# An attention-plus-FFN kernel whose engine orders are written out by a list scheduler in the kernel, with fp32 loads cast on Pool, batch 0 taken pair by pair, and four shared PSUM buffers

## The chip, the cores and the metric

One core of one Trainium2 chip. The metric is the device time of one execution in microseconds (us). Every execution has a state: "slow" when it is over 1.5% above the fastest of the same kernel, otherwise "fast". Engine names are those of the profile: PE (TensorE matmul), PEld (its weight load), DVE (VectorE), ACT (ScalarE), POOL (GpSimd), SP (SyncE, which here only issues DMAs; SPq is its queue).

## The reference

Block-sparse attention over 4 batches, 8 heads, 768 positions and 64 values a head, followed by a feed-forward network (FFN) on the 3072 x 512 result.

```python
scores = scale * q @ k.T                      # per batch and head
mask   = neighbours | first/last block | sampled_blocks   # blocks of 32
attn   = softmax(where(mask, scores, -1e9)); x = attn @ v
h = x @ w_in                                  # 3072 x 1024
e = exp(h - max); solu = h * e / sum(e)
ln = (solu - mean) / sqrt(var + 1e-6) * g_ln
out = ln @ w_out                              # fp32, 3072 x 512
```

Both kernels work in bf16. The mask is added by the score matmul itself: 24 extra rows of the transposed k hold a block selector ("selp" rows) and 24 extra rows of the transposed q hold the block mask ("mskp" rows). So no score can be computed before a short chain of small operations has built the mask from `sampled_blocks`. The layer norm's mean is folded into w_out once, at the start ("w_out preparation": scale by g, column sums on PE, scale and subtract).

The work comes in units of (batch, tile of 256 queries, pair of heads). A unit has 3 score tiles, 3 exps of 128x1024 and one P·V accumulation with a normalisation (`r`, `x`). Four units of one (batch, tile) give the x of one FFN block. There are 48 units, 144 exps and 12 FFN blocks.

## The kernel before

Tile buffers and their waits are handled by the framework; the order of instructions on each engine is the order of the program text.

```python
def load_pair(b, pr):                 # q, k, v of two heads: cast by the Pool's DMA
    for src, nm in ((k, "kc"), (q, "qc")):
        t = ld.tile([P, NCH, 2, D], BF16, tag=nm, name=nm)
        for hh in range(2):
            nc.gpsimd.dma_start(out=t[:, :, hh, :],
                in_=src[b, 2 * pr + hh, :, :].rearrange("(p c) d -> p c d", p=P))
    ...                               # v likewise
# ... mask chain: affine_selects on Pool, then on DVE samp_lo, eq, anyeq, maskT,
#     mskb, and the two permuted copies selp and mskp
def transpose_pair(b, pr):            # 6 PE transposes each of k and q, copied out by DVE
    ...
def prep_w1():                        # DVE: w_out_g[c] = w_out_f[c] * g[c], 8 times
def prep_w2():                        # PE column sums, then DVE, 8 times:
    nc.vector.scalar_tensor_tensor(out=w_out_sb[:, c, :], in0=w_out_f[:, c, :],
        scalar=g_sb[:, c:c+1], in1=wbar, op0=ALU.mult, op1=ALU.subtract)
# ... PSUM: 2 score tiles, 2 tiles "h", 2 tiles "m" for all else
units = [(b, t, pr) for b in range(B) for t in range(NT) for pr in range(NPR)]
for u, (b, t, pr) in enumerate(units):
    ...                               # loads and transposes of the next batch
    for n in range(3):
        scores(b, t, pr, n, exs)      # 4 matmuls, 1 exp
        if n == 0 and prev is not None:
            pv(*prev)
            # a finished (b, t) appends its FFN pieces to bg
        if bg: bg.popleft()()         # one FFN piece between score tiles
```

The softmax here doesn't subtract the row's maximum and nothing guards it: scores larger than these inputs give would overflow.

## Time and profile before

| | kernel before |
|---|---|
| time, median of 4 runs | 282.58 us (281.29 to 283.04) |
| profiled span | 281.1 us, clock 0.997 |
| first score matmul | 24.96 us |
| first FFN block's input copied (xT) | 50.94 us |
| PE busy | 85% |

The page of the kernel before. In the rows of 40 digits one digit is a fortieth of the span (7.0 us) and gives the busy share in tenths; the queue line gives packets, MB and the share of the 16 DMA engines' time; the last line is the chain of work that ended last, by engine.

```profile
span 281.1 us, 7445 instructions
PE 238.8 (85%) x3163; PEld 183.2 (65%) x3177; DVE 157.9 (56%) x365; ACT 174.4 (62%) x206; POOL 82.8 (29%) x142
...
PE   0116686999999999999999999999999999899783
...
ACT  1002468548858859667677688588488595785630
...
DMA  5999999409759810049279020090100200200202
...
q0 software_dynamic: 55056, 10.49, 45.8%
...
PE 62%; DMA 11%; ACT 10%; DVE 9%; issue 3%; POOL 3%; ACTq 0%; POOLq 0%
```

Seven slices of start, 27 in which PE is busy 90% or more, and a short end. The timeline of the same kernel (start, duration, engine, line, operation; "x8" is eight in a row; in brackets how long the engine was idle and what ended it):

```profile
2.21 0.12 DVE L110 CAST samp_lo<-samp_i 1x72 bf16<-1x72 int32 x1
...
13.11 0.80 PE L161 MATMUL tp<-ident,kc 128*128 128x128 bf16 x6 [10.51 <-DMA kc<-in_k_dram]
...
18.65 0.65 DVE L138 COPY selp<-sel 24x768 bf16<-24x768 bf16 x1
...
22.99 0.65 DVE L138 COPY mskp<-mskb 24x768 bf16<-24x768 bf16 x1
...
24.96 1.91 PE L215 MATMUL s<-qT_87,kT_85 88*128 88x256 bf16 x8
...
34.14 3.80 DVE L192 TENSOR_SCALAR w_out_g<-w_out_f,g_sb 128x512 bf16<-128x512 f32 x8
...
42.93 5.37 DVE L203 SCALAR_TENSOR_TENSOR w_out_sb<-w_out_f,g_sb,wbar 128x512 bf16<-128x512 f32 x8
```

The first k load releases PE at 13.11 us, the mask chain ends at 23.6 us, the first score follows at 24.96 us. Four durations here matter later: the undisturbed samp_lo takes 0.12 us, selp and mskp take 0.65 us each, and the two halves of the w_out preparation 3.80 and 5.37 us.

**How full is PE?** Busy PE is not full PE, so I count work. From gap-free pieces of this trace: 8 score matmuls take 0.89 us, 24 P·V matmuls 0.75, 8 h matmuls 0.875, 8 output matmuls 1.74, 8 statistics matmuls 0.20. The Trainium skill, "TensorE: Matmul & The Clock Gate" (section "Wait — 56ns, not 53.3ns?") gives N / 2.4 GHz plus about 2.5 ns from one warm matmul to the next, from which I estimate 109.2 ns for 256 columns; the trace agrees with 0.875 / 8 = 109.4 ns. A transpose of 128 columns is taken as 0.056 us by the same formula (an estimate). Work in a stretch is the number of weight loads of each kind in it times these paces, 216 us for the whole program; "lost" is the length of the stretch minus its work. These are estimates, good to about a microsecond.

| kernel before | length | work | lost |
|---|---|---|---|
| 0 to 66 us | 66 | 29.2 | 36.8 |
| 66 to 238 us | 172 | 155.6 | 16.4 |
| 238 to 281.1 us | 43.1 | 31.5 | 11.6 |

### The profile page before, as it was taken

To read this page: it belongs to the slowest core of one execution; us is meant where nothing else is said; L and a number is where in the kernel's file an instruction comes from. 1 tells how busy PE (TensorE), PEld (TensorE's weight loads), DVE (VectorE), ACT (ScalarE), POOL (GpSimd) and SP (SyncE) were. 2 spreads that over 40 slices of the span, in tenths; PEclk is the share of its full clock that TensorE was granted. 3 is DMA by queue.
4 is the path that set the end of the run, shared out by engine and by line. 5 is a ranking of instruction groups with operands and counts; after the bars stand their busy time and mean duration, and the time that the engine had idled before them with its cause. 6 is when DMAs were issued, how large, how long until landed. Compare 5 with 4: busy or idle time off the path is not lost.

```text
span 281.1 us, 7445 instructions
## 1 busy us (share of the span) xinstructions
PE 238.8 (85%) x3163; PEld 183.2 (65%) x3177; DVE 157.9 (56%) x365; ACT 174.4 (62%) x206; POOL 82.8 (29%) x142
## 2 busy tenths in 40 slices
PE   0116686999999999999999999999999999899783
PEld 0004564867867867867767768678678577686561
DVE  3079789648639622756666616386376236155261
ACT  1002468548858859667677688588488595785630
POOL 8695861218139110045253100140100101001001
PEclk9999999999999999999999999999999999999998
DMA  5999999409759810049279020090100200200202
GB/s 117 264 191 188 185 180 118 58 4 140 48 93 128 85 54 23 2 90 100 30 109 79 3 77 2 37 96 2 47 31 2 77 2 2 76 2 3 76 0 77
DMA packets 61636, 20.40 MB, mean 73 GB/s; under 512 B 52225, under 2 KB 56994, under 8 KB 61602
## 3 DMA queue, kind: packets, MB, share of 16 engines
q0 software_dynamic: 55056, 10.49, 45.8%
q1 hardware_dynamic: 6546, 9.43, 9.8%
q8 instruction: 25, 0.41, 0.6%
q14 instruction: 9, 0.07, 0.1%
HBM read 23.07 MB, written 6.29 MB: 104 GB/s over the span
## 4 chain that ended last, share of the span: by engine, by line
PE 62%; DMA 11%; ACT 10%; DVE 9%; issue 3%; POOL 3%; ACTq 0%; POOLq 0%
PE s L215 15%; PE h L268 15%; PE ops L304 14%; PE op L231 10%; ACT ex L220 8%; DMA kc<-in_k_dram 7%; PE s3p L283 6%; DMA vc<-in_v_dram 4%; DVE w_out_sb L203 2%; ACT ot L312 2%; PE tp L161 2%; POOL qc L73 1%; DVE xT L258 1%; PE tps L256 1%; DVE x L240 1%
## 5 line engine op out<-in xcount | busy, mean ns | idle before, releaser
L220 ACT ACTIVATE ex<-s 128x1024 bf16<-128x1024 f32 x144 | 141.1, 1024 | 68.9 <-PE s L215 67.8
L215 PE MATMUL s<-qT_87,kT_85 88*128 88x256 bf16 (+1 forms) x288 | 49.5, 284 | 5.8 <-ACT ex L220 3.1
L231 PEld LDWEIGHTS <-ex 128*128 128x128 bf16 x1152 | 45.7, 98 | 11.1 <-ACT ex L220 4.6
L268 PE MATMUL h<-xT,w_in_sb 128*128 128x256 bf16 x384 | 47.8, 272 | 1.3 <-DVE xT L258 0.6
L215 PE MATMUL s<-qT_88,kT_86 88*128 88x256 bf16 (+1 forms) x288 | 46.2, 272 | 2.0 <-ACT ex L220 1.2
L273 DVE TENSOR_TENSOR solu<-h,e 128x512 bf16<-128x512 f32 x48 | 33.0, 687 | 26.3 <-ACT e L272 26.2
L304 PE MATMUL ops<-w_out_sb,solu 128*128 128x512 bf16 x179 | 44.6, 378 | 0.9 <-DVE s_4734 L290 0.3
L268 PEld LDWEIGHTS <-w_in_sb 128*128 128x128 bf16 x384 | 37.0, 97 | 6.3 <-issue 1.6
L272 ACT ACTIVATE e<-h 128x512 bf16<-128x512 f32 x48 | 28.7, 598 | 18.1 <-PE h L268 16.9
L215 PEld LDWEIGHTS <-kT_85 88*128 88x128 bf16 (+1 forms) x288 | 27.3, 101 | 13.5 <-issue 6.0
L73 POOL DMA_DIRECT2D kc<-in_k_dram x32 | 26.8, 841 | 18.6 <-PE tp L161 17.7
L215 PEld LDWEIGHTS <-kT_86 88*128 88x128 bf16 (+1 forms) x288 | 26.0, 97 | 9.3 <-issue 4.0
L304 PEld LDWEIGHTS <-solu 128*128 128x128 bf16 x192 | 18.4, 97 | 18.1 <-issue 0.3
L73 POOL DMA_DIRECT2D qc<-in_q_dram x32 | 26.2, 822 | 8.0 <-DMA w_in_sb<-in_moe_w_in_dram 3.7
L231 PE MATMUL op<-va_92,ex 128*128 128x65 bf16 x576 | 26.2, 193 | 2.7 <-ACT ex L220 2.2
L231 PE MATMUL op<-va_91,ex 128*128 128x65 bf16 x576 | 25.2, 196 | 1.9 <-DVE x L240 1.0
L239 DVE RECIPROCAL r<-op 128x4 f32<-128x4 f32 x48 | 8.5, 180 | 30.8 <-PE op L231 29.3
L274 DVE TENSOR_TENSOR sq<-solu 128x512 bf16<-128x512 bf16 x48 | 20.4, 425 | 1.3
L240 DVE TENSOR_TENSOR x<-op,r 128x256 bf16<-128x256 f32 x48 | 20.1, 420 | 1.0
L161 PE MATMUL tp<-ident,kc 128*128 128x128 bf16 x96 | 9.2, 240 | 12.2 <-DMA kc<-in_k_dram 10.5
L309 DVE TENSOR_SCALAR ot<-ops,rs 128x512 f32<-128x512 f32 x12 | 9.0, 751 | 16.7 <-PE ops L304 12.7
L312 ACT ACTIVATE ot<-ops,rs 128x512 f32<-128x512 f32 x12 | 8.2, 687 | 14.3 <-PE ops L304 14.3
(127 smaller groups left out, 201.7 us busy)
## 6 DMA issues: line engine op xcount, KB each, us to landing
out_dram<-ot SPq DMA_DIRECT2D x24, 256.0 KB
kc<-in_k_dram POOLq DMA_DIRECT2D x32, 96.0 KB, 5.1
qc<-in_q_dram POOLq DMA_DIRECT2D x32, 96.0 KB, 4.4
vc<-in_v_dram POOLq DMA_DIRECT2D x16, 192.0 KB, 5.0
w_out_f<-in_moe_w_out_dram SPq DMA_DIRECT2D x1, 2048.0 KB
w_in_sb<-in_moe_w_in_dram POOLq DMA_DIRECT2D x1, 1024.0 KB, 9.5
kT_86<-selp SPq DMA_DIRECT2D x8, 36.0 KB
qT_88<-mskp SPq DMA_DIRECT2D x8, 36.0 KB
```

The lines of the kernel that those rows point to most:

```text
L73: nc.gpsimd.dma_start(out=t[:, :, hh, :], in_=src[b, 2 * pr + hh, :, :].rearrange("(p c) d -> p c d", p=P))
L161: nc.tensor.matmul(tp[:, c * P : (c + 1) * P], src[:, c, :, :], ident, is_transpose=True, start=(c == 0), stop=(c == NCH - 1))
L215: nc.tensor.matmul(s[:, m, :], kT[i][rows[hh], hh, pr, jc * P : (jc + 1) * P], qT[i][rows[hh], hh, pr, t * TW : (t + 1) * TW], start=(m % ...
L220: nc.scalar.activation(out=e, in_=s, func=ACT.Exp, scale=scale)
L231: nc.tensor.matmul(op[:, qt, hh, :], exs[n][:, m, qt * P : (qt + 1) * P], va[i][:, 2 * pr + hh, jc, :], start=first, stop=(n == 2 and m == ...
L240: nc.vector.tensor_tensor(out=x[:, :, 2 * pr * D : (2 * pr + 2) * D].rearrange("p a (h d) -> p a h d", h=2), in0=op[:, :, :, 0:D], in1=r.b ...
L268: nc.tensor.matmul(h[:, ff, :], w_in_sb[:, c, f * P : (f + 1) * P], st["xT"][:, c, :], start=(ff == 0 and c == 0), stop=(ff == 1 and c == ...
L272: nc.scalar.activation(out=st["e"][:, sl, :], in_=h, func=ACT.Exp)
L273: nc.vector.tensor_mul(out=st["solu"][:, sl, :], in0=h, in1=st["e"][:, sl, :])
L274: nc.vector.tensor_mul(out=st["sq"][:, sl, :], in0=st["solu"][:, sl, :], in1=st["solu"][:, sl, :])
L283: nc.tensor.matmul(s3p[:, qt, g : g + 1], st[nm][:, f, qt * P : (qt + 1) * P], onesf[:, 0:1], start=first, stop=(qt == 1 and g == 2 and f ...
L304: nc.tensor.matmul(ops, st["solu"][:, f, qt * P : (qt + 1) * P], w_out_sb[:, f, :], start=(f == 0), stop=(f == KF - 1))
```

## The change

Intent: start earlier, and leave PE no bubbles. Every instruction becomes an `op` with an estimated duration, dependencies and a due date (in units of exps). A greedy list scheduler gives each engine its order, and the kernel emits that order. Loads are plain fp32 DMAs with 1536-byte rows issued by SP, cast afterwards on Pool. (The Trainium skill, "DMA: Bandwidth & Descriptors", section "SWDGE vs HWDGE vs iDMA", says that only a DMA issued from Pool can cast on the way.) In batch 0 a pair of heads is used for all three tiles before the next pair is needed. The four PSUM buffers that are not for scores are shared by everything.

```diff
+class Plan:
+    def run(self):                       # greedy: the engine that can start first goes on
+        ...
+                for o in ops:
+                    t, slot = self.place(o)
+                    if t == INF: continue
+                    key = (max(t, now), o.due) if t > now + 0.02 else (now, o.due)
+                    if pick is None or key < pick[0]: pick = (key, o, slot, max(t, now))
-    ps_h = ctx.enter_context(tc.tile_pool(name="ps_h", bufs=2, space=PSUM))
-    ps_m = ctx.enter_context(tc.tile_pool(name="ps_m", bufs=2, space=PSUM))
+    mbank = [psum.tile([P, 2, TW], FP32, name=f"mbank{i}") for i in range(4)]
-            nc.gpsimd.dma_start(out=t[:, :, hh, :], in_=src[b, 2 * pr + hh, :, :]...)
+        stage[(which, b, pr)] = op("SP", 0.08, lambda o: nc.sync.dma_start(
+            out=dst[o.slot].rearrange("p h c d -> p h (c d)"),
+            in_=src[b, 2 * pr : 2 * pr + 2]...), due=-50 + len(loads), ...)
+            ca = op("POOL", pool_us(S), cast, [ld], due=due, ...)     # pool_us(768) = 0.89
+    zeros[(nm, i)] = op("POOL", ..., memset of kT/qT of the other pairs, due=-30 + 40 * i)
+    mask_rows[0].append(op("DVE", ..., rows of pairs 1 to 3 copied, due=-30))
+    w_out_f = (eso ... .bitcast(FP32))   # the fp32 w_out lies where e and solu come later
+    wg = [op("DVE", dve_us(d_model, 2), ..., due=20) for c in range(KF)]
+    wo = [op("DVE", dve_us(d_model), ..., [wb], due=28) for c in range(KF)]
-units = [(b, t, pr) for b in range(B) for t in range(NT) for pr in range(NPR)]
+units = [(0, t, pr) for pr in range(NPR) for t in range(NT)]
+units += [(b, t, pr) for b in range(1, B) for t in range(NT) for pr in range(NPR)]
+            feed(b, t, lambda f, j=j: 37 + 9.8 * (j + f))   # due dates of the FFN pieces
+    order = plan.run()
+    with tc.manual_schedule():
+        for o in order: o.emit(o)
```

## The prediction

> **What bounds it now.** The profile page has PE busy 85% of 281.1 us, ACT 62%, DVE 56%, POOL 29%; the chain of waits is 62% PE, 11% DMA. Two stages differ.
>
> Start (0 to 50 us): by the windows only 221 of 3163 matmuls have begun by 50 us. In the timeline the first scores start at 24.9 us: the first k load, cast by a Pool DMA in 256-byte pieces (q0: 55056 packets, 45.8% of the DMA engines' time), releases PE at 13.1 us, and the mask chain waits behind other DVE work until 18.6 us. Scores then stutter (16 of 144 exps by 50 us) on loads, mask-row DMAs, DVE copies and a 5.3 us w_out block on DVE.
>
> After 50 us PE is 94 to 98% busy in the windows, but busy PE is not full PE: one (batch, tile) block repeats every 19.1 to 19.9 us in the chain. Gap-free pieces in the timeline: 8 score matmuls 0.89 us, 24 PV 0.75, 8 h 0.875, 8 output 1.74, 8 stats 0.20. My estimate of all PE work from these: 144x0.445 + 48x0.75 + 48x0.875 + 24x1.74 + 72x0.20 + transposes about 16 + 2 = 216 us. So some 65 us are lost: 35 to 40 at the start, about 20 in bubbles (19.2 against about 17.5 per block), about 7 at the end.
>
> **What the change does.** (1) Loads become hardware-queue DMAs with 1536-byte rows; 80 Pool DMA issues of 0.72 to 0.84 us (64 us of Pool) go, 46 Pool casts of 768 columns come. The Pool select of 768 columns took 1.01 us, so about 48 us: off the path. The Trainium skill, "SBUF — State Buffer" (who interferes with whom) says a Pool op and a two-port DVE op exclude each other; no line of this trace shows it, but I expect some DVE ops (squares, casts) to lengthen. DVE has 40% idle. (2) The mask chain comes first, memsets move to Pool: first scores at about 9 us (estimate: load landed about 4, cast, transposes, about 8 us of DVE work). (3) Batch 0 pair by pair: each pair gives 9 exps. Back-to-back exps run at 0.92 us (5 in 4.69), so the 30 exps before the first FFN block end at about 9+28 = 37 us, ACT-bound, PE having done about 25 us of its work. (4) The order spreads FFN pieces between scores evenly, and four shared PSUM buffers replace 2+2: bubbles shrink.
>
> **Sum.** 37 + (216-25) + 6 for the last block's latency and output DMA + 5 of remaining bubbles = 239 us. ACT after 37 us needs only 114x0.92 + 48x0.5 + 12x0.6 = 136 us, so PE bounds the rest. Of the 43 us gained, about 25 come from the start, 15 from bubbles, the rest from the tail.
>
> Predicted 239 us; 230 to 251 holds it 8 times in 10. Faster by over 2%: 0.96; within 2%: 0.03; slower: 0.01.
>
> **What would show each step.** First score at 8 to 11 us. ACT nearly gapless to about 37 us, with PE about half used, then PE over 95% in every slice. Block repeat 16.5 to 17.8 us. Chain: PE 75 to 80%, DMA under 5%, ACT 10% or more at the start. Pool casts 0.9 to 1.2 us. Under-512-byte packets fall from 52225 to a few thousand. Matmul and exp durations unchanged, clock about 1.0.
>
> **What would make it wrong.** Pool casts much slower than 1 us (staging buffers and SP's in-order queue stall loads, and outputs behind them); DVE blocked by Pool, delaying solu and so PSUM release; the fixed order built on durations that differ from the chip's, so that an in-order engine waits where another order would not (blocks stay at 19 us: about 255); a first score later than 9 us.

## The result

| | before | changed |
|---|---|---|
| time, median of 4 runs | 282.58 us | 257.42 us (256.93 to 259.12) |
| profiled span, clock | 281.1 us, 0.997 | 255.2 us, 0.99 |
| first score matmul | 24.96 us | 16.95 us |
| first xT copy | 50.94 us | 65.92 us |
| PE busy | 85% | 88% |

The ratio is 0.9128 (0.9085 to 0.917). A ratio is the mean time of one kernel's fast runs over that of the other's of the same rounds, so it is not quite the ratio of the medians. The kernel is 8.7% faster, and 18 us above the prediction; the range 230 to 251 does not hold it.

The page of the changed kernel (one digit is now 6.4 us):

```profile
span 255.2 us, 7442 instructions
PE 223.4 (88%) x3155; PEld 182.7 (72%) x3177; DVE 159.3 (62%) x329; ACT 175.7 (69%) x210; POOL 66.8 (26%) x120
...
PE   0539778984999999999999999999999999999692
...
ACT  3218899696548958588686884877959688686331
...
DMA  6999999999234041022110200202002020100202
...
q1 hardware_dynamic: 19024, 27.86, 33.2%
...
PE 73%; DVE 16%; ACT 6%; issue 2%; POOL 1%; POOLq 0%; ACTq 0%
```

DMA has left the chain (11% before, absent now), DVE has grown in it from 9% to 16%. Of the seven slices from 19 to 64 us five are still below 9 in PE's row, and from there on all are 9 up to the tail. The DMA row is full for nine slices, from 6 to 64 us: the staging loads run far ahead of their use.

The windows of the changed kernel, cut at the first score, at the first xT copy and at 238 us (length, busy us and instructions of each engine, clock, DMA share, GB/s):

```profile
0.00:17.00 17.00, 3.36 (x26) 2.55 (x27) 15.43 (x24) 3.94 (x5) 15.66 (x33) 1.00 0.91 296
17.00:66.00 49.00, 39.43 (x539) 32.31 (x539) 37.46 (x71) 38.90 (x41) 22.87 (x25) 0.97 1.04 313
66.00:238.00 172.00, 170.67 (x2473) 141.01 (x2491) 100.13 (x223) 128.54 (x159) 27.00 (x59) 1.00 0.14 47
238.00:255.20 17.20, 9.92 (x127) 6.85 (x125) 6.31 (x13) 4.35 (x7) 1.27 (x4) 0.95 0.14 54
```

and with work counted as before:

| changed kernel | length | work | lost |
|---|---|---|---|
| 0 to 17 us | 17 | 1.6 | 15.4 |
| 17 to 66 us | 49 | 33.3 | 15.7 |
| 66 to 238 us | 172 | 172.1 | -0.1 |
| 238 to 255.2 us | 17.2 | 9.3 | 7.9 |

So the 26 us of span came from the bubbles (16.4 lost before, none now), the tail (11.6 to 7.9), and only 6 from the start (36.8 to 31.1). The start was to give 25.

Where the start goes is in the timeline. First the mask chain, then the stretch before the first xT:

```profile
2.61 1.73 DVE L298 COPY selp<-sel 24x768 bf16<-24x768 bf16 x1 [0.37 <-POOL sel L270]
...
2.80 1.62 POOL L265 TENSOR_SCALAR_AFFINE_SELECT maskT<-maskT 24x24 f32<-24x24 f32 x1
...
4.28 2.34 DVE L277 CAST samp_lo<-samp_i 1x72 bf16<-1x72 int32 x1
4.37 1.05 POOL L314 MEMSET kT<- 64x1152 int32 x1
...
5.52 1.05 POOL L314 MEMSET qT<- 64x1152 int32 x1
...
8.27 1.34 DVE L320 COPY kT<-selp 24x2304 bf16<-24x2304 bf16 x1
...
13.18 2.82 DVE L298 COPY mskp<-mskb 24x768 bf16<-24x768 bf16 x1
13.39 0.82 POOL L374 CAST qb<-qst 128x768 bf16<-128x768 f32 x1
14.16 1.37 POOL L314 MEMSET kT<- 64x1536 int32 x1
...
16.95 0.58 PE L425 MATMUL sbank<-qT,kT 88*128 88x256 bf16 x2 [5.18 <-DVE qT L308]
...
36.67 11.72 ACT L431 ACTIVATE ex<-sbank 128x1024 bf16<-128x1024 f32 x12 [0.43 <-PE sbank L425]
...
42.64 5.78 DVE L343 TENSOR_SCALAR sqall<-eso,g_sb 128x512 bf16<-128x512 f32 x8
...
48.97 0.60 ACT L352 ACTIVATE wbar<-mbank 128x512 f32<-128x512 f32 x1 [0.58 <-PE mbank L349]
...
51.02 3.10 ACT L431 ACTIVATE ex<-sbank 128x1024 bf16<-128x1024 f32 x3 [1.46 <-PE sbank L425]
...
55.69 2.64 DVE L354 SCALAR_TENSOR_TENSOR w_out_sb<-eso,g_sb,wbar 128x512 bf16<-128x512 f32 x3
...
61.52 1.12 DVE L399 COPY qT<-mbank 64x768 bf16<-64x768 bf16 x2
62.68 0.25 DVE L452 RECIPROCAL r<-mbank 128x4 f32<-128x4 f32 x2
...
65.92 0.69 DVE L480 COPY xT<-mbank 128x1024 bf16<-128x1024 bf16 x1 [1.06 <-PE mbank L476]
```

Two things stand out. The DVE operations of the mask chain are three to twenty times longer than before, each beside a Pool operation: selp 1.73 us (0.65), samp_lo 2.34 us (0.12), mskp 2.82 us (0.65). Two row copies for pairs 1 to 3, 1.34 and 1.33 us, run in the middle of the chain as well. And from 42.6 to 62.6 us DVE has almost nothing but the w_out preparation and the copies of batch 1's transposed k and q. The reciprocals of finished units wait behind them, and with them the first FFN block. The 30th exp, the last that this block needs, is the first of the three at 51.02 us.

The scheduler's own plan tells how far its model is off. It is a calculation inside the kernel, not a measurement. It has the first score at 10.7 us, the first xT copy at 52.6 and the end at 239.3. Forty exps stand before that xT copy in the plan, and 40 had begun before it on the chip. The chip is 13.3 us behind at the xT copy and 15.9 at the end of the span, so nearly all the delay arises before 66 us.

### The profile page after: what moved, and what is told of

Its sections match the earlier page's. It is cut to its first block, busy times and chain, and to the rows that moved or that the text cites. A ratio compares the mean times of both kernels' runs of the same rounds, so it can differ in the third digit from the quotient of the medians.

```text
span 255.2 us, 7442 instructions
## 1 busy us (share of the span) xinstructions
PE 223.4 (88%) x3155; PEld 182.7 (72%) x3177; DVE 159.3 (62%) x329; ACT 175.7 (69%) x210; POOL 66.8 (26%) x120
## 2 busy tenths in 40 slices
DMA packets 19587, 29.39 MB, mean 115 GB/s; under 512 B 2273, under 2 KB 14946, under 8 KB 19554
## 3 DMA queue, kind: packets, MB, share of 16 engines
q0 software_dynamic: 528, 1.05, 2.2%
## 4 chain that ended last, share of the span: by engine, by line
PE 73%; DVE 16%; ACT 6%; issue 2%; POOL 1%; POOLq 0%; ACTq 0%
PE sbank L425 21%; PE mbank L494 15%; PE mbank L547 14%; PE mbank L442 12%; PE mbank L520 6%; ACT ex L431 5%; PE mbank L383 3%; DVE w_out_sb L354 3%; DVE sqall L343 2%; PE mbank L476 2%; DVE kT L399 2%; DVE qT L399 1%; DVE mskp L298 1%; DVE kT L320 1%; DVE eso L506 1%
## 5 line engine op out<-in xcount | busy, mean ns | idle before, releaser
L431 ACT ACTIVATE ex<-sbank 128x1024 bf16<-128x1024 f32 x144 | 141.9, 1026 | 45.7 <-PE sbank L425 44.9
L425 PE MATMUL sbank<-qT,kT 128*128 128x256 bf16 (+1 forms) x576 | 84.3, 277 | 11.3 <-ACT ex L431 5.6
L425 PEld LDWEIGHTS <-kT 128*128 128x128 bf16 (+1 forms) x576 | 53.7, 99 | 23.6 <-issue 14.6
L494 PE MATMUL mbank<-xT,w_in_sb 128*128 128x256 bf16 x384 | 48.1, 273 | 0.8 <-DVE xT L480 0.8
L442 PE MATMUL mbank<-va,ex 128*128 128x65 bf16 x1152 | 44.4, 195 | 2.9 <-DVE qT L399 1.8
L506 DVE TENSOR_TENSOR eso<-mbank,eso 128x512 bf16<-128x512 f32 x48 | 32.7, 687 | 20.0 <-ACT eso L502 19.6
L547 PE MATMUL mbank<-w_out_sb,eso 128*128 128x512 bf16 x170 | 43.4, 379 | 1.7 <-DVE eso L506 0.5
L502 ACT ACTIVATE eso<-mbank 128x512 bf16<-128x512 f32 x48 | 28.8, 602 | 9.3 <-PE mbank L494 9.3
L510 DVE TENSOR_TENSOR sqall<-eso 128x512 bf16<-128x512 bf16 x48 | 21.1, 446 | 0.9
L455 DVE TENSOR_TENSOR x<-mbank,r 128x256 bf16<-128x256 f32 x48 | 20.1, 421 | 1.2
```

Of the source, the lines that this page charges most:

```text
L425: nc.tensor.matmul(s[:, m, :], kT[i][rows[hh], hh, pr, jc * P : (jc + 1) * P], qT[i][rows[hh], hh, pr, t * TW : (t + 1) * TW], start=(m % ...
L431: exs.append(op("ACT", act_us(1024), lambda o, so=so: nc.scalar.activation(out=exb[o.slot], in_=sbank[so.slot], func=ACT.Exp, scale=scale) ...
L442: nc.tensor.matmul(acc[:, qt, hh, :], exb[exs[n].slot][:, m, qt * P : (qt + 1) * P], va[i][:, 2 * pr + hh, jc, :], start=first, stop=(n == ...
L455: nrm = op("DVE", dve_us(TW), lambda o: nc.vector.tensor_tensor(out=xb[x_of[(b, t)].slot][:, :, 2 * pr * D : (2 * pr + 2) * D].rearrange(" ...
L494: nc.tensor.matmul(h[:, ff, :], w_in_sb[:, c, f * P : (f + 1) * P], xTb[xc.slot][:, c].rearrange("p a q -> p (a q)"), start=(ff == 0 and c ...
L502: e = op("ACT", act_us(512), lambda o, h=h, sl=sl: nc.scalar.activation(out=eb[(es[0] if es else o).slot][:, sl, :], in_=mbank[h.slot], fu ...
```

## The experiments

Theory A: in the first 17 us Pool's zeroing and casting holds up DVE's mask chain (together with row copies that the greedy order puts first). Theory B: DVE's w_out preparation before the first FFN block delays that block. Rivals: the pair-by-pair order of batch 0 itself, whose first FFN block needs ten units; PE's in-order transposes for batch 1; the load queue. For the part that went well: is it the order or the PSUM layout that took the bubbles away?

Fifteen runs on the chip, in four groups that each shared a chip and the runs of the kernel before (medians 282.17 to 282.75 us). To compare two experiments, the difference of their ratios is multiplied by 282.5 us. All were correct except four.

### 1. quiet_pool: the orders kept, but Pool silent at the start

The plan is the same; Pool's zeroings and casts that it puts before 14 us are issued on ACT.

```diff
+    for o in order:
+        if o.eng == "POOL" and o.start < 14 and o.kind in ("cast", "zero"):
+            o.eng = "ACT"
```

> The order of PE, DVE and SP is kept exactly; the Pool zeroing and Pool casts that the plan starts before 14 us are issued on ACT instead, where ACT was idle. Theory A (Pool and DVE shut each other out of SBUF, and that is why the first scores came at 16.95 us and not at about 9 to 11): the DVE permute of the key mask (1.73 us after, 0.65 before), samp_lo (2.34 against 0.12) and the permute of the query mask (2.82 against 0.65) fall to 0.9, 0.3 and 0.9 us or less, the first score comes at 13.5 us or earlier, and the time falls by 2 to 5 us to about 253 to 255. Rival (the load traffic of about 300 GB/s slows DVE, or these ops are simply long in this place): durations and first score stay within 10%, time 256 to 259.

Measured: 260.0 us, ratio 0.9219. The mechanism of A is confirmed: with Pool quiet selp takes 0.84 us, samp_lo 0.20, mskp 0.66, and the first score comes at 13.51 us instead of 16.95:

```profile
3.39 0.20 DVE L278 CAST samp_lo<-samp_i 1x72 bf16<-1x72 int32 x1
...
11.15 0.66 DVE L299 COPY mskp<-mskb 24x768 bf16<-24x768 bf16 x1
```

The time is not better but 2.6 us worse, and the first xT copy stays at 66.34 us. ACT, which has to deliver the exps next, got a zeroing of 2.75 us at 19.31 us and casts of 0.82 and 0.83 us between its first exps. The granted clock of these runs is also lower (0.978 to 0.985, against 0.99 of the changed kernel), so part of the 2.6 us may be that. This measures the mechanism, not what it costs.

### 2. no_wprep: the w_out preparation left out (wrong)

The raw w_out comes by a casting DMA; the 16 DVE operations, the column sums and wbar go; all other orders stay.

```diff
+        nc.gpsimd.dma_start(out=w_out_sb, in_=moe_w_out.rearrange("(c p) d -> p c d", p=P))
+    gone = set(map(id, wg + wo + [cs, wb]))
+    order = [o for o in order if id(o) not in gone]
```

> Wrong result on purpose: the w_out preparation (8 scalings and 8 scale-and-subtract on DVE, 8 matmuls, one ACT op) is left out and w_out is loaded raw by a casting DMA; all orders else are kept. Theory B (the first FFN block comes at 66 us and not at 37 to 45 because DVE's fixed order puts the w_out preparation, about 13 us with its delays, ahead of the normalisations that the FFN and the PSUM buffers wait for): the first xT copy (65.9 us) comes at 59 us or earlier, the time falls by 4 to 8 us to 249 to 253. Rival (what gates it is the exps of ACT and the late first score): first xT copy at 63 us or later, time 255 to 258.

Measured: 251.57 us (one of four runs slow), ratio 0.8907; first score 17.09 us, xT copy 60.15 (1 us later than B asked).

```profile
60.15 0.69 DVE L483 COPY xT<-mbank 128x1024 bf16<-128x1024 bf16 x1 [0.24 <-PE mbank L479]
```

The preparation costs 6 us: so much less than the changed kernel, by an edit that before the first score adds only one DMA issue on Pool (0.90 us at 12.12 us). Whether its place in DVE's order costs this, as B says, or the work itself, this run cannot tell; run 5 asks that. A part may be clock: in the changed kernel the window from 62.4 to 65.8 us has a granted clock of 0.50, close to PE waits of 1.57 and 1.80 us for DVE copies; no_wprep has 1.00 there. The kernel still reads the fp32 w_out, so it reads w_out twice; I took that for harmless here, and it was not (run 12).

### 3. quiet_no_wprep: both edits (wrong)

The edits of 1 and 2 together.

> Both edits together, wrong result on purpose, orders kept. If the two losses are separate they add: first score at 13.5 us or earlier, first xT copy at 55 us or earlier, time about 245 to 249. If they are the same slack, the time equals that of the better one alone, 249 to 253. The kernel's own plan, which knows neither delay, ends at 239 us.

Measured: 255.23 us, ratio 0.905; first score 13.50 us, xT copy 64.55. The expected sum did not come. ACT has the same additional load as in run 1, and w_out is read twice as in run 2, so the run cannot say whether A and B add.

### 4. psum_split: two PSUM buffers for h, two for the rest

The plan is made again with two pools of two in place of the one of four.

```diff
-    plan.pool("m", 4)
+    plan.pool("m", 2)
+    plan.pool("h", 2)
```

> The order is written by the same scheduler, but the four shared PSUM buffers are split again into 2 for h and 2 for all else, as in the kernel before. Theory C (the written order removed the bubbles of the steady stage, the PSUM layout little): blocks repeat in 15.7 to 16.5 us, time within 3 us of 257.4. Rival (the four shared buffers did): blocks repeat in 17 us or more, time 264 us or more. The scheduler's own plan puts the split 6 us later (245 against 239), so near 263 would say that the plan is right about it.

Measured: 263.92 us, ratio 0.936, 6.5 us above the changed kernel. The scheduler's plan had said 6 us (245.4 against 239.3). The loss sits where it should: 7.4 us lost between 66 and 240 us (none with four shared), with a block every 16.5 us instead of 15.9, and a similar start (15.3 and 13.7 us lost in the two windows up to 66). Of the 16.4 us of bubbles that went, about 7 are then due to the shared buffers under this scheduler, and the other 9 to the rest of the change, the order above all. That rest includes 40 exps done before the first FFN block, which leaves fewer exps beside each block; the two were not separated. Which other orders would do with two and two was not tried.

### 5. early_w: w_out prepared early, in a buffer of its own

```diff
-    w_out_f = (eso ... .bitcast(FP32) ...)
+    w_out_f = const.tile([P, KF, d_model], FP32, name="w_out_f")
-    ... w_out load after stage[("v", 1, 0)], dues wg 20, cs 24, wo 28
+    ... w_out load after stage[("v", 0, 3)], dues wg -8, cs 2, wo 4
```

> w_out gets a buffer of its own (it shared the bytes of e and solu), is loaded after the 12 loads of batch 0 instead of after 15, and its preparation is due early, so that the first FFN no longer waits for it; the result is correct. Theory B (DVE's w_out preparation ahead of the normalisations holds up the first FFN): first xT copy at 59 us or earlier (65.9 after, 60.2 without the preparation), time 250 to 253. Rival (what counted in the run without the preparation was the 13 us of DVE work itself, not its place in the order): first xT copy at 62 us or later, time 255 to 258.

Measured: 255.73 us, ratio 0.9032, 2.7 us below the changed kernel; first score 18.13 us, xT copy 61.80. (Its profiled run was a slow one, clock 0.977, so its trace is read only coarsely.) Between the two expectations, and the interval (0.8973 to 0.9091) overlaps that of the changed kernel: inconclusive. So it is not shown that the preparation's place, and not its work, costs the 6 us of run 2. The preparation stays on DVE, so it presumably delays something else.

### 6. start_fix: only the start's order mended

Nothing moves to another engine. Pool's zeroing and DVE's row copies for pairs 1 to 3 come after the mask chain, and the scheduler may wait up to 0.6 us for an urgent operation instead of taking whatever is ready. (Three small Pool operations of the start are shifted too, and the plan is made again.)

```diff
-   key = (max(t, now), o.due) if t > now + 0.02 else (now, o.due)
+   key = (max(t, now), o.due) if t > now + (0.6 if o.due <= -76 else 0.02) else (now, o.due)
-   zeros ...   due=-30 + 40 * i)
+   zeros ...   due=-30 + 40 * i, after=[p2, sels])
-   mask_rows[0] ...  due=-30)
+   mask_rows[0] ...  due=-30, after=mask_rows0)
```

> Only the start's order is changed, nothing moves to ACT: Pool's zeroing and the DVE mask rows of pairs 1 to 3 come after the mask chain of the first scores. Theory A: the permutes of the masks take 0.9 us or less and the first score comes at 12 us or earlier (16.95 after, 13.5 with the zeroing and casts on ACT). If an earlier first score is worth its microseconds (and the quiet Pool run was slower only because it loaded ACT, which bounds the stage that follows), the time falls to 251 to 254. Rival: the first FFN is gated elsewhere and swallows the gain; time 256 to 258.

Measured: 251.3 us, ratio 0.8883: 7 us below the changed kernel. Its timeline:

```profile
2.43 0.66 DVE L298 COPY selp<-sel 24x768 bf16<-24x768 bf16 x1 [0.24 <-POOL sel L270]
...
3.08 0.17 DVE L277 CAST samp_lo<-samp_i 1x72 bf16<-1x72 int32 x1
...
6.52 0.66 DVE L298 COPY mskp<-mskb 24x768 bf16<-24x768 bf16 x1
...
10.89 1.01 PE L425 MATMUL sbank<-qT,kT 88*128 88x256 bf16 x4 [2.79 <-DVE qT L399]
```

The three operations are back at their undisturbed durations, the first score comes 6 us earlier (10.89 us; 16.95 in the changed kernel), and the time falls by about as much. By the work count 10.1 us are lost before the first score (15.4 in the changed kernel) and 15.3 from there to 66 us (15.7), so the gain lies where A puts it. This confirms A, with its cost. It does not divide that cost between Pool's interference and the row copies, since both were mended; in quiet_pool, where the row copies stay, 3.4 of the 6 us of first score had gone.

### 7. early_start: 5 and 6 together

> Both of the edits of early_w and start_fix. If the two losses add: first score at 12 us or earlier, first xT copy at 54 us or earlier, time 245 to 249. If they share one slack, it equals the better of the two, 250 to 253.

Measured: 252.09 us (two of four runs slow), ratio 0.8849; first score 9.60 us, xT copy 55.37. The sum was missed; it is what was expected if both edits share one slack. It is no clear gain over start_fix alone (0.8883, intervals overlap). DVE waits 5.86 us, in order, for the w_out load to land at 32.52 us. Then the interference turns up with the roles exchanged:

```profile
40.58 5.37 DVE L353 SCALAR_TENSOR_TENSOR w_out_sb<-w_out_f,g_sb,wbar 128x512 bf16<-128x512 f32 x8
40.80 5.85 POOL L373 CAST kb<-kst 128x768 bf16<-128x768 f32 x1 [1.14 <-DMA kst<-in_k_dram]
```

A Pool cast that takes 0.82 us undisturbed takes 5.85 us beside eight back-to-back DVE operations.

### 8. early_tmajor: early_w with batch 0 tile by tile

```diff
-    units = [(0, t, pr) for pr in range(NPR) for t in range(NT)]
+    units = [(0, t, pr) for t in range(NT) for pr in range(NPR)]
```

> early_w with one part of the change undone: batch 0 again tile by tile and not pair by pair, so that the first FFN's inputs are complete after 12 exps and not 30. If pair by pair itself holds the first FFN back: first xT copy at 45 us or earlier and a time at least 3 us below early_w. Rival (tile by tile makes all four pairs' preparation on DVE due at once, and the exps wait for it): time equal to early_w or longer.

Measured: 253.82 us, ratio 0.8984; xT copy 47.82 us. The rival asks for at least 3 us against early_w (0.9032); the difference is 1.4 us with overlapping intervals. The first FFN block comes 14 us earlier, and the time hardly moves: within the noise of some 3 us, which unit comes first is not what costs the time. The moment of the first xT copy alone is therefore no measure of the start.

### 9. start_no_wprep: 6 and 2 together (wrong)

> start_fix and the run without w_out preparation together; wrong result on purpose. Each alone took about 6 us off 257.4. If they are two separate losses they add: first score near 11 us, first xT copy at 54 us or earlier, time 244 to 247. If they share one slack: 249 to 252.

Measured: 251.35 us, ratio 0.8893; the sum (244 to 247) was missed by over 4 us. With A and B both taken away, nothing was gained over A alone. Pool waited 13.4 us for a single k load in this run. That pointed to the second reading of w_out.

### 10 and 11. replan_pair and replan_tile: the scheduler with a mended model

The model gets durations nearer to the traces (DVE overhead 0.15 us, Pool cast 0.82, SP issue 0.4, loads at 300 GB/s), and an exclusion: Pool operations and those DVE operations that the runs had shown to suffer may not overlap in the plan. The fp32 w_out has its own buffer and is loaded after the first six loads; start_fix's start is kept; due dates were chosen by the plan's end. 11 takes batch 0 tile by tile.

```diff
+        self.lock = eng == "POOL" and load is None
+        if o.lock: t = max(t, self.lock_free)
+    for o in [slo, p1, p2, any2, any3, *mask_rows0, *mask_rows[0], *wg, *wo, *two_port]:
+        o.lock = o.eng == "DVE"
-            feed(b, t, lambda f, j=j: 37 + 9.8 * (j + f))
+            feed(b, t, lambda f, j=j: 43 + 9.5 * (j + f))
```

> A version meant to be better, correct: start_fix's start; w_out in its own buffer and loaded after 6 loads so that DVE need not wait for it; and the scheduler's model mended from the traces: longer DVE durations, SP issues of 0.4 us, loads at 300 GB/s, w_out landing later, and Pool and two-port DVE operations never planned at the same time; due dates chosen by that plan (its end: 236 us). Expected 244 to 249, below start_fix by 2 us or more, with no DVE or Pool operation stretched over 3 us. Rival (a mended model makes the order no better, because what remains is ACT's rate and the last block): 250 to 253.

> The same mended scheduler with batch 0 tile by tile, as in the kernel before (its plan ends at 236 us as well). If pair by pair is of no use once the start and w_out are mended, within 2% of replan_pair, 243 to 250; if tile by tile overloads DVE at the start, 252 or more.

Measured: 247.22 us, ratio 0.8739 (first score 13.98 us, xT copy 55.26), and 245.97 us, ratio 0.8692 (15.31 and 43.92). Both correct, 11 and 12 us below the changed kernel. The first score is later than in start_fix: in the tile version two mask-row copies took 3.59 us together beside Pool (0.35 us each undisturbed), so the start was not mended well here. As many things change at once, these runs give a better version, not a cause.

### 12. start_no_wprep2: run 9 without the fp32 reading of w_out (wrong)

```diff
-    gone = set(map(id, wg + wo + [cs, wb]))
+    gone = set(map(id, wg + wo + [cs, wb, w_out_load, g_load]))
```

> The run of the two edits together once more, without its flaw: that kernel read w_out twice (2 MB more of loads in a stage in which the DMA engines were full), so this one leaves out the fp32 read. Wrong result on purpose. If the failed addition (251.3, as each edit alone) came from the load queue (batch 1's first k arrived late, and the PE order has its transposes ahead of batch 0's scores): PE busy from 30 to 50 us at 16 us or more (11.0 there), time 244 to 248. If the two losses really share one slack: 250 to 252.

Measured: 242.89 us, ratio 0.8605, 8.1 us below run 9. The windows of 30 to 50 us, first of start_no_wprep:

```profile
30.00:40.00 10.00, 4.77 (x72) 3.72 (x71) 0.79 (x3) 6.95 (x8) 0.00 (x0) 1.00 1.10 336
40.00:50.00 10.00, 6.26 (x77) 5.45 (x78) 3.17 (x7) 3.36 (x4) 4.98 (x6) 0.66 1.05 299
```

and of start_no_wprep2:

```profile
30.00:40.00 10.00, 8.32 (x127) 6.92 (x127) 3.95 (x10) 9.12 (x11) 3.32 (x4) 1.00 1.15 268
40.00:50.00 10.00, 8.69 (x148) 7.79 (x147) 5.65 (x14) 8.69 (x10) 5.46 (x7) 1.00 1.07 311
```

PE, 11.0 of 20 us busy with the additional 2 MB, is busy 17.0 without them; Pool's stretch of ten microseconds without a cast is gone. Two things follow. First, A and B add at least for the most part: with both gone and w_out read once, the ratio falls by 0.052 (15 us), where A alone gave 7 and B alone, with its double reading, 6. The sum is not clean: this run also takes the w_out load (and the 4 KB of g) out of SP's queue, where the changed kernel has it. Second, loads can be a limit of their own: 2 MB more of them cost 8 us in this order. The DMA engines are full in both runs (1.05 to 1.15), so what differs is what stands in the queue. In run 9 SP's issue of w_out lasts 7.36 us and that of batch 1's first k load, behind it, 6.92. A Pool cast waited 13.4 us for that k load, PE's transposes of batch 1 waited 7.3 us for that cast, and ACT waited 7.7 us for the score behind them. Part of the 8 us is clock: run 9's granted clock was 0.50 from 40.8 to 47.6 us (hence the 0.66 above), which includes 4.5 us of PE work, so some 2 us at most (an estimate from these figures).

### 13. start_late_tp: start_fix with batches 1 to 3 transposed later

```diff
-            prepare(b, pr, 9 * pr - 40 if b == 0 else 36 * b - 27 + 6 * pr)
+            prepare(b, pr, 9 * pr - 40 if b == 0 else 36 * b - 10 + 3 * pr)
```

> start_fix with one number changed: the transposes and copies of batches 1 to 3 are due about 17 exps later, so that PE and DVE are not set to do batch 1's preparation while batch 0 runs. If that preparation (waiting for loads, and filling DVE between 40 and 60 us) is the third thing that holds the first FFN back: first xT copy at 54 us or earlier (57.6 in start_fix), time 246 to 249. Rival: no change, 250 to 252.

Measured: 250.65 us (one slow run), ratio 0.8912 against start_fix's 0.8883, intervals overlapping. The first xT copy comes at 53.36 us (57.62 in start_fix), as early as was asked, and the time does not follow: no difference to be seen within some 3 us. The moment of that copy is again no measure.

### 14 and 15. replan2_pair and replan2_tile: the re-plan with its start mended

Casts and zeroings of other pairs may start only once the first pair's mask rows are begun; the exclusion is not applied in the first 8 us; w_out's preparation and the normalisations are due earlier.

```diff
-    zeros ... after=[p2, sels])
+    zeros ... after=mask_rows0)
-    ca = op(e, us, cast, [ld], due=due, take=mp, last_of=[ld])
+    ca = op(e, us, cast, [ld], due=due, take=mp, last_of=[ld], after=[] if first else mask_rows0)
```

> replan_pair with a start in which Pool's zeroing and casts of the other pairs come only after the first pair's mask rows (they stretched the last mask copies to 3.6 us there): first score at 12 us or earlier (14.0 there), no DVE operation of the start over 1 us but the long row copies, time 242 to 246 (247.2 there). Rival (the first score no longer matters because the loads bound the stage after it): 246 to 248.

> The same with batch 0 tile by tile: first score at 12 us or earlier (15.3), time 241 to 245 (246.0 without). Rival as above: 245 to 247.

Measured: 244.25 us, ratio 0.8659, and 243.52 us (242.34 to 244.11), ratio 0.862 (0.8582 to 0.8658). Both correct. The tile version beats the kernel before by 13.8% and the changed one by 5.6% (0.862 / 0.9128). Its page:

```profile
span 241.8 us, 7461 instructions
PE 221.3 (92%) x3177; PEld 181.3 (75%) x3177; DVE 150.5 (62%) x329; ACT 175.2 (72%) x210; POOL 65.0 (27%) x120
...
PE   0498788899999999999999999999999999999892
```

Its first score comes at 11.11 us. Counted in work it loses 12.1 us up to 17 us and 7.5 from 17 to 66 (15.4 and 15.7 in the changed kernel), nothing up to 225, and 6.1 in the tail. Pair by pair against tile by tile is 244.25 against 243.52 us: no clear difference again.

## Why the prediction was wrong

Predicted 239 us, measured 257.42. The sum was 37 + 191 + 6 + 5. Term by term:

**The step that failed: "the 30 exps before the first FFN block end at about 9+28 = 37 us, ACT-bound, PE having done about 25 us of its work".** PE was full only from about 66 us, with 34.9 us of work done (1.6 + 33.3). That is 66 - 34.9 = 31.1 us lost, where the prediction had 37 - 25 = 12: an error of 19 us, as much as the whole miss (19 more here, 5 less for the bubbles, 2 more for the tail, and 2 between span and time). Of the 31.1 us, 15.4 are lost before the first score, 9.8 from there to the end of the 30th exp, and 5.9 from there to 66 us. Reaching the full PE took 29 us longer (66 instead of 37), of which 10 are given back as work already done (35 instead of 25). The 29 us fall into three parts, by the timeline:

- *"First scores at about 9 us"*: 16.95 us, 8 us late. The estimate of "about 8 us of DVE work" presumably took the durations of the kernel before, where Pool was doing other things. Beside Pool's zeroing and casting the same operations were three to twenty times longer. Shown by quiet_pool (the durations come back when Pool is quiet) and start_fix (first score 10.89 us, 7 us of time gained). The prediction had named the mechanism, from the Trainium skill, "SBUF — State Buffer" (section "Who interferes with whom"), but expected it in the squares and casts, and gave it no microseconds. In the steady stage it is indeed small: the squares went from a mean of 425 to 446 ns.
- *30 exps in 28 us*: from 16.95 us to the end of the 30th exp at 52.05 us is 35 us, 7 more. Here "ACT-bound" was nearly right and its size wrong. From 18.00 to 48.39 us ACT ran 29 exps in 30.4 us and waited only 2.2 us for scores (the line at 36.67 us has twelve of them). Of the 7 us, about 1 passes between the first score and the first exp, 1.5 come from exps of 0.97 us on average where 0.92 was taken, 2.2 are those waits, and 2.6 come before the 30th exp, where ACT waits for the column sums (0.58 us), makes wbar (0.60) and waits for a score (1.46). These last belong to the w_out preparation. Loads hardly show in this stretch: Pool waited 10.0 us for k loads, but no wait of ACT or PE between 18 and 48 us is longer than 0.73 us. That the changed kernel's own single reading of w_out costs time through its place in the queue was not tested alone.
- *The FFN starts when the 30th exp is done*: 14 us passed between that exp and the first xT copy. The written order does not start it there: the first block is due at exp 37 (`feed`, in the diff), and 40 exps had begun before the xT copy, in no_wprep as well, where 9.8 us still passed. The prediction did not read this from the change. This delay is not all loss, since PE has scores and P·V to do meanwhile (early_tmajor and start_late_tp: an earlier xT copy, the same time). The other 4 us, and the 1.7 us by which the 30th exp is earlier in no_wprep, are the w_out preparation. The prediction left it out of the sum, although it had noted "a 5.3 us w_out block on DVE" in the old profile. In the changed kernel its DVE pieces, 5.78 us and about 7 us, stand before the reciprocals that the first FFN block needs. Shown by no_wprep: 6 us less, xT copy at 60.15 us. That its place and not its work is what costs is not shown (early_w).

With A and B gone and w_out read once (run 12) the time is 242.89 us, 4 us from the prediction and inside its range. That nearness is in part luck: by the work count run 12 still loses 18.5 us up to 66 us, where the prediction had 12, and the bubbles (0.9 lost where 5 were predicted) give most of it back.

**The bubbles.** Predicted to shrink from about 20 to 5; measured 16.4 to none by the work count. Right, and better by 5. psum_split gives about 7 of the 16 to the shared buffers and leaves 9 to the rest, the order above all. The block repeat was predicted at 16.5 to 17.8 us and was 15.9. That is not a faster PE: durations are unchanged (h matmul 273 ns mean, 272 before; exp 1026 ns, 1024 before). At 66 us already 40 of 144 exps were done and no FFN block, so the 12 blocks share 104 exps, and a block comes with about 9 exps instead of 12.

**The tail.** Predicted 6 us; 7.9 lost. About right.

**The DMA and Pool terms.** Right. Packets under 512 bytes fell from 52225 to 2273, DMA left the chain, the casts took 876 to 941 ns on average (predicted 0.9 to 1.2 us). That these casts are "off the path" held for Pool's own time but not for what they did to DVE.

**The chain.** PE 73% (predicted 75 to 80), DMA none (under 5%), ACT 6% (10% or more at the start): the missing share went to DVE, 16%, the engine of both unpriced causes.

The prediction's list of what would make it wrong had these causes in part: DVE blocked by Pool, an order built on durations that differ from the chip's, a first score later than 9 us. They stood beside the sum and not in it, and the range allowed 12 us for causes that came to 18.

## What to carry to other kernels

A fixed order is only as good as the durations it is built on, and durations measured in one kernel are not those of another in which different engines overlap: before moving work to Pool, ask which DVE operations of a critical chain will run beside it. Price one-time work, such as a weight preparation, on the engine where it stands in order before something urgent; idle share over the whole span says nothing about it. A greedy scheduler that takes whatever is ready puts non-urgent work ahead of an urgent operation that would be ready a fraction of a microsecond later; a small look-ahead and a few order constraints at the start were worth 7 us here, where the steady stage had nothing left to give.

## What the Trainium skill lacked or had wrong

- "SBUF — State Buffer", section "Who interferes with whom", says that Pool and certain DVE operations exclude each other, and that the loser blocks for the whole instruction of the winner. The traces agree in kind, but the wait can be far longer than one instruction: a 1x72 DVE cast (0.12 to 0.20 us alone) lasted 2.34 us, across two Pool zeroings of 1.05 us and a selection, and a Pool cast (0.82 us alone) lasted 5.85 us, across eight back-to-back DVE operations of 5.37 us in all. A rule for a run of back-to-back operations on the other engine is missing. No run here shows which port or mode each operation used.
- Two of the same section's exemptions held: DVE copies out of PSUM kept their 0.55 us beside Pool, and a DVE reduction took 0.21 us (0.22 before) during a Pool cast.
- "GPSIMD Engine Reference", section "Elementwise — side-by-side cycle accounting", has figures for additions and loops, none for a plain fp32 to bf16 cast: 128x768 took 0.82 us undisturbed.
- "DMA: Bandwidth & Descriptors", section "Latency and other measured facts", does not say how long SP is held by issuing a load while the DMA engines are full. Here 0.37 to 0.5 us for most of the 384 KB loads, and 4.66 us for a load of 2 MB and 4.20 us for the 384 KB load after it (DMA share 1.10 from 18 to 28 us). For a kernel that plans SP's order this is a term of the plan.
